# The first four row tiles of x: turned by TensorE, or by transposing transfers from SP

## The chip, the cores and the metric

One core of a Trainium2 chip. The metric is the device time of one execution in microseconds (us). The profile adds the span, from the first instruction of the program that it records to the last.

## The reference

Two linear-attention blocks, A and B, read the same x (2048 rows, D = 640, 32 heads of 20). B's own x is not used. Per block, in bf16:

```python
qkv = x @ wqkv                           # 640 -> 3 * 640
phi = lambda t: jnp.where(t > 0, t + 1, jnp.exp(t)) + 1e-6
pq, pk = phi(q), phi(k)
kv = jnp.einsum("bhsd,bhse->bhde", pk, v)
z = jnp.einsum("bhsd->bhd", pk)
o = (pq @ kv) / (pq . z + 1e-6)          # per head
block = o @ wo
```

The result mixes them by a gate: `g = sigmoid((x * gate_w).sum(-1))`, `out = g * a + (1 - g) * b`.

## The kernel before

The 2048 rows are 16 row tiles (chunks) of 128 and four row blocks of 512 (n = 0 to 3); the 640 columns of x are five slices of 128 (c = 0 to 4). Two copies of x lie in SBUF: `xn`, rows on partitions, and `xT`, columns on partitions (five slices of 2048). The products with wk and wq contract over columns and read `xT`; the later passes that build x^T pk (`g_pass`, `g_strassen`) read `xn`.

**What PE does, in order.** Seven warm-up matmuls on a constant (L172). The transpose of the gate row `grow` (5 x 128, in a corner of the tile `R`) into `gcol` (L174); DVE copies it to `gsb` and GpSimd puts it as a 641st column behind each slice of wkA (L178), so that the second k matmul of each slice (321 columns) also gives the gate's logits. Then `k_first` (L252), whose order is written out by hand: the first four chunks of `xn` are transposed on TensorE (`x_transpose`, L215), four times five transposes, and DVE copies the result into `xT` (L218, two copies for each chunk). Then k for chunks 0 to 3: 40 matmuls (L236; five slices, two halves of 320 columns, four chunks), slice 0 for all, slice 1 for all, then slices 2 to 4 chunk by chunk. `k_done` ends a chunk: ACT's exp (L223) and a copy of the logit column (L242), DVE's two operations of phi (L228, L232).

After that come q for row block 0 (`q_block` twice, `q_single`; L296, L306), k for chunks 4 to 7, q for block 1, k for the other chunks, q for blocks 2 and 3 (L285), and the later passes: the sums of x and pk, x^T pk by Strassen's scheme, the normalisers, all of B, and the output products (L607).

PSUM is held in four slots of two banks (`ps`, tags ps0 to ps3). The warm-up and `gcol` have slot 3, the turned chunks slots 0 and 1; the k products of chunks 0 to 3 have slots 2, 3, 0, 1.

**What the queues do.** SP and ACT issue the first transfers. ACT: the gate row, x tiles 1 and 3, wkA slice 1. SP: x tiles 0 and 2, wkA slice 0, slice 2, slices 3 and 4, then wqA in two parts (L136), then 15 transposing transfers (L139), which write `xT` for row blocks 1 to 3 straight from DRAM, five slices of 512 columns for each block. Later on SP: x rows of blocks 1 to 3 into `xn` (L738), wvA, woA (L695), wkB.

In row block 0, tile q holds the rows 4p + q (p = partition), and the stores of the result (`rows_of`) undo this.

Transfers of the hardware queues take turns on eight completion semaphores: the ninth waits for the landing of the first, and so on, on the queue that issues it.

GpSimd makes the constants first (identity, masks, `spread`, `I16`), then the gate columns, then clears part of `R` and fills `chosen`, both for a later pass.

Of the kernel before, what the change touches and what calls it, by code (L numbers as in the profile page):

```python
# [8 lines left out]
P = 128  # L9
FP32 = mybir.dt.float32  # L10
BF16 = mybir.dt.bfloat16
# [3 lines left out]
S, D, H = 2048, 640, 32  # L15
Dh = D // H
DT = D // P
ST = S // P
NB = 4
CB = 4  # L20
HB = 512
# [12 lines left out]
def kernel(  # L34
# [11 lines left out]
    nc = tc.nc  # L46
    x2 = A_x.flatten_outer_dims()
    out2 = out.flatten_outer_dims()
# [4 lines left out]
    work = ctx.enter_context(tc.tile_pool(name="work", bufs=2))  # L53
# [18 lines left out]
    xn = persist.tile([P, ST, D], BF16, name="xn")  # L72
# [6 lines left out]
    ident = persist.tile([P, P], BF16, name="ident")  # L79
# [5 lines left out]
    R = persist.tile([P, 2, 4, RB], BF16, name="R")  # L85
    ones = persist.tile([P, H], BF16, name="ones")
    I16 = persist.tile([P, ST], BF16, name="I16")
# [3 lines left out]
    hc, ic = ST // 2, 2 * P  # L91
# [14 lines left out]
    wq_dram = [A_wqkv.rearrange("(c p) f -> p c f", p=P), B_wqkv.rearrange("(c p) f -> p c f", p=P)]  # L106
# [3 lines left out]
    nc.vector.memset(ones[:], 1.0)  # L110
    nc.vector.memset(KVT[:], 0.0)
    nc.vector.memset(lift[:], 1.0 + EPS)
    xb0 = x2[0:CB * P, :].rearrange("(p q) d -> p q d", q=CB)
    wk = [None, None]
    wv = [None, None]
    wq = [None, None]
    wk[0] = wpool.tile([P, DT, D + 16], BF16, tag="wk", name="wkA")
    def load_x(eng, lo, hi):
        eng.dma_start(out=xn[:, lo:hi, :], in_=xb0[:, lo:hi, :])

    def load_wk(eng, lo, hi):
        eng.dma_start(out=wk[0][:, lo:hi, 0:D], in_=wq_dram[0][:, lo:hi, D:2 * D])

    grow, logitT = R[0:DT, 0, 2, 0:P], R[:, 0, 1, 0:P]
    nc.scalar.dma_start(out=grow, in_=gate_w.rearrange("(c p) -> c p", p=P))
    load_x(nc.sync, 0, 1)
    load_x(nc.scalar, 1, 2)
    load_x(nc.sync, 2, 3)
    load_x(nc.scalar, 3, 4)
    load_wk(nc.sync, 0, 1)  # L130
    load_wk(nc.scalar, 1, 2)
    load_wk(nc.sync, 2, 3)
    load_wk(nc.sync, 3, DT)
    wq[0] = wpool.tile([P, DT, D], BF16, tag="wq", name="wqA")
    for lo, hi in ((0, 2), (2, DT)):
        nc.sync.dma_start(out=wq[0][:, lo:hi, :], in_=wq_dram[0][:, lo:hi, 0:D])  # L136
    for n in range(1, NB):
        for c in range(DT):
            nc.sync.dma_start_transpose(  # L139
                out=xT[:, c, n * HB:(n + 1) * HB], in_=x2[n * HB:(n + 1) * HB, c * P:(c + 1) * P]  # L140
            )


    make_identity(nc, ident[:])
    for r in range(4):
        rows = slice(32 * r, 32 * r + 32)
        nc.gpsimd.tensor_copy(out=I4[rows], in_=ident[rows, rows])
    nc.gpsimd.tensor_copy(
        out=spread[:].rearrange("p (h t) -> p h t", t=TW), in_=I4[:, :, None].to_broadcast([P, H, TW])
    )  # L150
    nc.gpsimd.tensor_tensor(
        out=I16[0:2 * ST], in0=ident[0:2 * ST, 0:ST], in1=ident[0:2 * ST, ST:2 * ST], op=ALU.add
    )
    nc.gpsimd.memset(maskE[:], 1.0)
    for sign, base in ((1, 0), (-1, Dh - 1)):
        nc.gpsimd.affine_select(
            out=maskE[:], in_=maskE[:], pattern=[[-sign * Dh, WB[0] // Dh], [0, Dh]],
# [3 lines left out]
    for sign, base in ((1, 0), (-1, TW - 1)):  # L161
        nc.gpsimd.affine_select(
            out=headE[:], in_=headE[:], pattern=[[-sign * TW, H]],
# [1 line left out]
        )  # L165


    raw = ps_raw("warm", 3)
    warm = raw.bitcast(FP32).rearrange("p (b n) -> p b n", b=2)
    one_l, one_r = [nc.const_aps.tensor(1.0, [P, n], BF16) for n in (P, HB)]  # L170
    for k in range(7):
        nc.tensor.matmul(warm[:, 0, :], lhsT=one_l, rhs=one_r, start=True, stop=True)  # L172
    gcol = raw[:, 2 * HB:2 * HB + DT]
    nc.tensor.transpose(out=gcol, in_=grow, identity=ident[0:DT, 0:DT])  # L174
    gsb = work.tile([P, DT], BF16, tag="rT", name="gsb")
    nc.vector.tensor_copy(out=gsb[:], in_=gcol)
    for c in (0, 1, 2, 4, 3):
        nc.gpsimd.tensor_copy(out=wk[0][:, c, D:D + 1], in_=gsb[:, c:c + 1])  # L178

    def by_group(dst, lhsT, src, h):  # L180

# [27 lines left out]

    def gate_done(b):  # L210
        nc.vector.tensor_scalar(ge[b][:], ge[b][:], 1.0, 1e30, op0=ALU.add, op1=ALU.min)

    def x_transpose(i, pt, cuts=(0, DT)):
        for c in range(DT):
            nc.tensor.transpose(out=pt[:, c * P:(c + 1) * P], in_=xn[:, i, c * P:(c + 1) * P], identity=ident[:])  # L215
        src = pt[:, 0:D].rearrange("p (c n) -> p c n", c=DT)
        for lo, hi in zip(cuts, cuts[1:]):
            nc.vector.tensor_copy(out=xT[:, lo:hi, i * P:(i + 1) * P], in_=src[:, lo:hi])  # L218

    def phi(dst, src, n, lifted=False, side=None):  # L220

        e = work.tile([P, src.shape[1], n], BF16, tag="e", name="e", bufs=3)
        nc.scalar.activation(out=e[:], in_=src, func=ACT.Exp)  # L223
        if side is not None:
            side()
        if lifted:
            nc.scalar.activation(out=dst, in_=src, func=ACT.Identity, bias=lift[:])
        nc.vector.tensor_scalar(e[:], e[:], 1.0, EPS, op0=ALU.min, op1=ALU.add)  # L228
        if lifted:
            nc.vector.tensor_tensor(out=dst, in0=dst, in1=e[:], op=ALU.max)  # L230
            return
        nc.vector.scalar_tensor_tensor(out=dst, in0=src, scalar=1.0 + EPS, in1=e[:], op0=ALU.add, op1=ALU.max)  # L232

    def k_mm(b, i, c, pt, hf):
        w = HF + (hf if b == 0 else 0)
        nc.tensor.matmul(  # L236
            pt[:, hf, 0:w], lhsT=xT[:, c, i * P:(i + 1) * P], rhs=wk[b][:, c, hf * HF:hf * HF + w],
            start=(c == 0), stop=(c == DT - 1),
        )

    def k_done(b, i, pt):
        side = (lambda: nc.scalar.copy(out=logit[:, i:i + 1], in_=pt[:, 1, HF:HF + 1])) if b == 0 else None  # L242
        phi(pk[:, i, :].rearrange("p (b n) -> p b n", b=2), pt[:, :, 0:HF], HF, side=side)

    def k_chunk(b, i, slot=None):
        pt = ps(f"k{'AB'[b]}", slot)
        for hf in range(2):
            for c in range(DT):
                k_mm(b, i, c, pt, hf)
        k_done(b, i, pt)  # L250

    def k_first():  # L252

        pts = [ps("kA", 2 + i) for i in range(2)]
        raw = [ps_raw("xt", i) for i in range(2)]

        def part(i, cs):
            for c in cs:
                for hf in range(2):
                    k_mm(0, i, c, pts[i], hf)  # L260

        for i in range(4):
            x_transpose(i, raw[i % 2][:, i // 2 * 2 * HB:], (0, 2, DT))
        for i in range(2):
            part(i, (0,))
        pts += [ps("kA", i) for i in range(2)]
        for i in range(2, 4):
            part(i, (0,))
        for i in range(4):
            part(i, (1,))  # L270
        for i in range(4):
            part(i, (2, 3, 4))
            k_done(0, i, pts[i])

    def mixed(t, m):
# [320 lines left out]
        nc.vector.tensor_tensor(out=pqT[b][:, m, :], in0=pqT[b][:, m, :], in1=rec, op=ALU.mult)  # L596

    def rows_of(i):
        n, q = divmod(i, CB)
        rows = out2[n * HB:(n + 1) * HB, :]  # L600
        return rows.rearrange("(p q) d -> q p d", q=CB)[q] if n == 0 else rows[q * P:(q + 1) * P, :]

    def prod(dst, left, right, i, first):

# [12 lines left out]
    class Pair:  # L617
# [7 lines left out]
        def store(self, k, lo=0, hi=D):  # L625
            eng = nc.scalar if self.last and k else nc.sync
            eng.dma_start(out=rows_of(self.i + k * (ST // 2))[:, lo:hi], in_=self.osb[k][:, lo:hi])
# [89 lines left out]
    with tc.manual_schedule():  # L717
        k_first()
    turn[0] = 2
    nc.gpsimd.memset(R[:, :, 0:2, :], 0.0)  # L720
    chosen = R[:, 1, 0:2, :].rearrange("p a (b n) -> p (a b) n", b=2)
    for h in range(2):
        for q in range(2):
            i0 = h * hc + q
            nc.gpsimd.tensor_copy(
                out=chosen[0:2 * ST, 2 * h + q, :].rearrange("p (j n) -> p j n", j=4),
                in_=I16[0:2 * ST, i0:i0 + hc - 1:2][:, :, None].to_broadcast([2 * ST, 4, 32]),
            )
    for n in range(2):
        for i in range(CB if n else 0, CB * 2 * n):  # L730
            k_chunk(0, i)
# [2 lines left out]
        q_single(0, DT - 1, n)  # L734
    for i in range(hc, ST - 2):
        k_chunk(0, i)
    for n in range(1, NB):
        nc.sync.dma_start(  # L738
            out=xn[:, n * CB:(n + 1) * CB, :], in_=x2[n * HB:(n + 1) * HB, :].rearrange("(q p) d -> p q d", p=P)
        )  # L740
    wv[0] = load_w(0, "v", nc.sync)
    load_wo(0, nc.sync)
# [5 lines left out]
    def bank(pool, name, n=1):  # L748
        return pool.tile([P, HB] if n == 1 else [P, n, HB], FP32, tag=name, name=name)

    with tc.manual_schedule():
# [31 lines left out]
        part = [slice(n * RB, (n + 1) * RB) for n in range(4)]  # L783
# [17 lines left out]
        with late_pool("single") as single:  # L801
# [6 lines left out]
            pts = [bank(single, f"s4{hf}")[:, 0:HF] for hf in range(2)]  # L808
# [21 lines left out]
        for i in range(1, half):  # L830
            p, after = pairs[i], pairs[i + 1] if i + 1 < half else None
# [9 lines left out]
            q = after if i + 2 < half else p if after is None else None  # L841
# [43 lines left out]
```

## Time and profile before

| | |
|---|---|
| time, median of 3 runs | 188.69 us (188.54 to 188.95) |
| the profiled execution | 188.86 us |
| its span | 187.2 us |
| busy: PE, DVE, ACT, POOL | 183.1, 150.3, 76.3, 6.0 us |
| first k matmul, first q matmul of PE | 6.43, 11.97 us |
| last of wqA landed | 10.8 us |

The profile's chain is the work that ended last, followed back from the end. Times in it are us from the span's start. Matmuls overlap in the engine, so a row's duration for one matmul is longer than the distance between two starts; where one matmul's cost is meant, the distance counts. "DMA to landing" is the time from the start of an issue to the completion semaphore. DMA share is the mean busy share of 16 DMA engines; it passes 1 where pieces that are waiting in the engines count as busy. PEld is the weight load, which runs beside the matmul before it.

### The profile page before, as it was taken

The page shows a single profiled execution, that of the slowest core. Times are in us where ns is not written, and L with a number is a line of the kernel's source. Part 1 is how long each engine was busy: PE and PEld are TensorE (multiplying, and loading weights), DVE is VectorE, ACT ScalarE, POOL GpSimd, SP SyncE. Part 2 cuts the span into 40 slices and gives each one's busy share as a digit, 9 for nine tenths or more (in the row PEclk, how much of TensorE's full clock was granted, in tenths as well). Part 3 has the DMA queues.
Part 4 walks back from the last instruction along what each step waited for, and adds up shares of the span by engine and source line. Part 5 has one row for each costly group of instructions (what it writes and reads, how often), then busy time and mean ns, then how long its engine had stood idle before and what let it go on. Part 6 is the DMA issues. An engine that isn't in the chain of part 4 may idle for free.

```text
span 187.2 us, 3548 instructions
## 1 busy us (share of the span) xinstructions
PE 183.1 (98%) x1426; PEld 123.7 (66%) x1431; DVE 150.3 (80%) x247; ACT 76.3 (41%) x124; POOL 6.0 (3%) x30
## 2 busy tenths in 40 slices
PE   8999999999999999999999999999999999999993
PEld 3765757765577677877775555576777776777772
DVE  1468868889998998799889998739699989787554
ACT  2065545547962501367674577432401611111120
POOL 7400000010000000000000000000000000000000
PEclk9999999999999999999999999999999999999999
DMA  5993449972040000011115000000533002311132
GB/s 169 323 165 74 99 98 352 322 164 101 9 170 0 0 4 0 0 36 33 55 38 190 8 0 0 0 4 0 179 98 77 4 0 91 123 67 65 50 107 70
DMA packets 19173, 15.64 MB, mean 84 GB/s; under 512 B 8916, under 2 KB 19028, under 8 KB 19156
## 3 DMA queue, kind: packets, MB, share of 16 engines
q1 hardware_dynamic: 18426, 14.75, 28.0%
q10 hardware_dynamic: 730, 0.66, 1.1%
q8 instruction: 11, 0.18, 0.4%
q14 instruction: 6, 0.05, 0.1%
HBM read 10.00 MB, written 3.44 MB: 72 GB/s over the span
## 4 chain that ended last, share of the span: by engine, by line
PE 96%; DVE 2%; issue 0%; ACT 0%; DVEq 0%; ACTq 0%
PE gs L367 16%; PE kA L236 12%; PE kB L236 12%; PE qB L285 12%; PE ox L607 6%; PE qA L285 6%; PE oy L607 5%; PE oz L607 5%; PE qA L296 5%; PE ow L607 3%; PE gA L340 2%; PE gB L340 2%; PE warm L172 2%; PE qA L306 1%; DVE osb L612 1%; PE xt L215 1%
## 5 line engine op out<-in xcount | busy, mean ns | idle before, releaser
L236 PEld LDWEIGHTS <-xT 128*128 128x128 bf16 x320 | 31.1, 98 | 12.4 <-DVE xT L218 0.2
L228 DVE TENSOR_SCALAR e<-e 128x640 bf16<-128x640 bf16 (+2 forms) x53 | 18.9, 357 | 8.3 <-ACT e L223 7.6
L236 PE MATMUL kB<-wkB,xT 128*128 128x320 bf16 x160 | 23.0, 299 | 0.0
L236 PE MATMUL kA<-wkA,xT 128*128 128x320 bf16 (+1 forms) x160 | 22.4, 300 | 0.0
L285 PE MATMUL qB<-xT,wqB 128*128 128x512 bf16 x98 | 21.7, 379 | 0.1
L223 ACT ACTIVATE e<-kB 128x640 bf16<-128x640 f32 x16 | 11.3, 705 | 18.8 <-PE kB L236 17.5
L285 PEld LDWEIGHTS <-wqB 128*128 128x128 bf16 x100 | 11.7, 117 | 9.8 <-issue 0.2
L223 ACT ACTIVATE e<-kA 128x640 bf16<-128x640 f32 x16 | 11.3, 705 | 13.4 <-PE kA L236 13.3
L232 DVE SCALAR_TENSOR_TENSOR pk<-kA,e 128x640 bf16<-128x640 f32 x16 | 13.2, 824 | 2.1 <-DVE e L228 0.2
L232 DVE SCALAR_TENSOR_TENSOR pk<-kB,e 128x640 bf16<-128x640 f32 x16 | 13.2, 825 | 1.7
L223 ACT ACTIVATE e<-qB 128x1024 bf16<-128x1024 f32 x10 | 10.3, 1025 | 8.7 <-PE qB L285 8.3
L223 ACT ACTIVATE e<-qA 128x1024 bf16<-128x1024 f32 (+1 forms) x11 | 10.4, 948 | 8.1 <-PE qA L296 5.1
L651 ACT COPY u<-ox 128x320 f32<-128x320 f32 x8 | 3.4, 427 | 21.8 <-PE ox L607 21.8
L367 PEld LDWEIGHTS <-S 128*128 128x128 bf16 x96 | 9.4, 98 | 3.6
L367 PEld LDWEIGHTS <-xn 128*128 128x128 bf16 x96 | 9.1, 98 | 4.0 <-issue 0.4
L285 PE MATMUL qA<-xT,wqA 128*128 128x512 bf16 x49 | 10.9, 379 | 0.1
L635 ACT COPY p1s<-ox 128x320 f32<-128x320 f32 x8 | 3.4, 427 | 16.5 <-PE ox L607 16.5
L607 PEld LDWEIGHTS <-xT 128*128 128x128 bf16 x85 | 8.0, 98 | 3.1 <-DVE xT L546 0.2
L607 PEld LDWEIGHTS <-pqTA 128*128 128x128 bf16 x85 | 7.9, 98 | 2.9 <-issue 0.2
L607 PEld LDWEIGHTS <-pqTB 128*128 128x128 bf16 x80 | 7.8, 98 | 3.0
L367 PE MATMUL gs<-pk,xn 128*128 128x320 bf16 x64 | 9.4, 300 | 0.0
L612 DVE TENSOR_TENSOR osb<-oz,u 128x320 bf16<-128x320 f32 (+1 forms) x18 | 8.0, 452 | 1.5 <-PE oz L607 0.8
(138 smaller groups left out, 293.6 us busy)
## 6 DMA issues: line engine op xcount, KB each, us to landing
out_dram<-osb SPq DMA_DIRECT2D x14, 160.0 KB, 1.8
xn<-in_A_x_dram SPq DMA_DIRECT2D x3, 640.0 KB, 6.6
wvA<-in_A_wqkv_dram SPq DMA_DIRECT2D x1, 800.0 KB, 10.6
wkB<-in_B_wqkv_dram SPq DMA_DIRECT2D x1, 800.0 KB, 4.5
wqB<-in_B_wqkv_dram SPq DMA_DIRECT2D x1, 800.0 KB, 4.6
MA<-ma_dram SPq DMA_DIRECT2D x1, 800.0 KB, 5.0
wvB<-in_B_wqkv_dram SPq DMA_DIRECT2D x1, 800.0 KB, 4.6
woB<-in_B_wo_dram SPq DMA_DIRECT2D x1, 800.0 KB, 5.7
```

Source lines behind the costliest of these rows:

```text
L172: nc.tensor.matmul(warm[:, 0, :], lhsT=one_l, rhs=one_r, start=True, stop=True)
L223: nc.scalar.activation(out=e[:], in_=src, func=ACT.Exp)
L228: nc.vector.tensor_scalar(e[:], e[:], 1.0, EPS, op0=ALU.min, op1=ALU.add)
L232: nc.vector.scalar_tensor_tensor(out=dst, in0=src, scalar=1.0 + EPS, in1=e[:], op0=ALU.add, op1=ALU.max)
L236: nc.tensor.matmul(pt[:, hf, 0:w], lhsT=xT[:, c, i * P:(i + 1) * P], rhs=wk[b][:, c, hf * HF:hf * HF + w], start=(c == 0), stop=(c == DT - 1),
L285: nc.tensor.matmul(pt[:, u, :], lhsT=mixed(wq[b][:, c, :], m), rhs=xT[:, c, n * HB:(n + 1) * HB], start=(c == 0), stop=(c == DT - 1),)
L296: nc.tensor.matmul(pt[:, u, :], lhsT=mixed(wq[b][:, c, :], m + u), rhs=xT[:, c, n * HB:(n + 1) * HB], start=(c == 0), stop=(c == DT - 1),)
L340: nc.tensor.matmul(pt[:, hf, 0:HF], lhsT=xn[:, i, c * P:(c + 1) * P], rhs=pk[:, i, hf * HF:(hf + 1) * HF], start=(i == 0), stop=(i == ST - 1),
L367: nc.tensor.matmul(pt[:, n, 0:HF], lhsT=left[:, i, n * P:(n + 1) * P], rhs=right[:, i, :], start=(first and i == 0), stop=(i == hc - 1), s ...
L607: nc.tensor.matmul(dst, lhsT=left[:, c, r0:r0 + P], rhs=right[:, c, :], start=(first and c == 0), stop=(c == DT - 1), skip_group_check=not ...
L612: nc.vector.tensor_tensor(out=dst, in0=acc, in1=sb, op=ALU.add)
L635: nc.scalar.copy(out=self.p1s[:], in_=self.at("x"))
```

## The change

Only row tile 0 of x is loaded to `xn` at the start and goes through TensorE: five transposes, three DVE copies with the one of the gate column between them. Rows 128 to 511 come transposed, by five transfers of 384 columns that are the first that SP issues. x tile 0 is the first on ACT; behind it all of wkA in three transfers (slice 0; 1 and 2; 3 and 4) and wqA's slices 0 and 1. wqA's slices 2 to 4 are on SP after the five. The gate row is loaded by GpSimd, and its transpose on PE stands behind those of x.

The order of the k matmuls in `k_first` changes: slice 0 by halves, chunks 1, 2, 3, 0; slice 1 for all chunks; the rest of chunk 0, which is then ended; slices 2, 3, 4 for chunks 1 to 3, each ended after its slice 4. The warm-up and `gcol` have slot 1, the turned tile slot 2. Clearing `R` and filling `chosen` moves into `k_first`, behind the gate columns on GpSimd. Rows are in plain order everywhere, so `rows_of` is simple; rows 128 to 511 are loaded into `xn` with the other blocks' rows, in a transfer of their own before theirs.

```diff
-    xb0 = x2[0:CB * P, :].rearrange("(p q) d -> p q d", q=CB)
-    def load_x(eng, lo, hi):
-        eng.dma_start(out=xn[:, lo:hi, :], in_=xb0[:, lo:hi, :])
+    def x_turned(c, lo, hi):
+        nc.sync.dma_start_transpose(out=xT[:, c, lo:hi], in_=x2[lo:hi, c * P:(c + 1) * P])
...
-    nc.scalar.dma_start(out=grow, in_=gate_w.rearrange("(c p) -> c p", p=P))
-    load_x(nc.sync, 0, 1)
-    load_x(nc.scalar, 1, 2)
-    load_x(nc.sync, 2, 3)
-    load_x(nc.scalar, 3, 4)
-    load_wk(nc.sync, 0, 1)
-    load_wk(nc.scalar, 1, 2)
-    load_wk(nc.sync, 2, 3)
-    load_wk(nc.sync, 3, DT)
...
-    for lo, hi in ((0, 2), (2, DT)):
-        nc.sync.dma_start(out=wq[0][:, lo:hi, :], in_=wq_dram[0][:, lo:hi, 0:D])
+    nc.gpsimd.dma_start(out=grow, in_=gate_w.rearrange("(c p) -> c p", p=P))
+    nc.scalar.dma_start(out=xn[:, 0, :], in_=x2[0:P, :])
+    for c in range(DT):
+        x_turned(c, P, HB)
+    for lo, hi in ((0, 1), (1, 3), (3, DT)):
+        load_wk(nc.scalar, lo, hi)
+    for eng, lo, hi in ((nc.scalar, 0, 2), (nc.sync, 2, DT)):
+        eng.dma_start(out=wq[0][:, lo:hi, :], in_=wq_dram[0][:, lo:hi, 0:D])
     for n in range(1, NB):
         for c in range(DT):
-            nc.sync.dma_start_transpose(
...
+            x_turned(c, n * HB, (n + 1) * HB)
...
-    raw = ps_raw("warm", 3)
+    raw = ps_raw("warm", 1)
...
     def k_first():
...
+        xt = ps_raw("xt", 2)
+        for c in range(DT):
+            nc.tensor.transpose(out=xt[:, c * P:(c + 1) * P], in_=xn[:, 0, c * P:(c + 1) * P], identity=ident[:])
+        nc.tensor.transpose(out=gcol, in_=grow, identity=ident[0:DT, 0:DT])
+        gsb = work.tile([P, DT], BF16, tag="rT", name="gsb")
+        src = xt[:, 0:D].rearrange("p (c n) -> p c n", c=DT)
+        nc.vector.tensor_copy(out=xT[:, 0:2, 0:P], in_=src[:, 0:2])
+        nc.vector.tensor_copy(out=gsb[:], in_=gcol)
+        nc.vector.tensor_copy(out=xT[:, 2:DT, 0:P], in_=src[:, 2:DT])
+        for c in range(DT):
+            nc.gpsimd.tensor_copy(out=wk[0][:, c, D:D + 1], in_=gsb[:, c:c + 1])
...
+        pts = {i: ps("kA", (2 + i) % 4) for i in (1, 2, 3, 0)}
+        for hf in range(2):
+            for i in (1, 2, 3, 0):
+                k_mm(0, i, 0, pts[i], hf)
...
-        for i in range(4):
-            x_transpose(i, raw[i % 2][:, i // 2 * 2 * HB:], (0, 2, DT))
...
+        for i in range(CB):
             part(i, (1,))
-        for i in range(4):
-            part(i, (2, 3, 4))
+        part(0, (2, 3, 4))
+        k_done(0, 0, pts[0])
+        for i in range(1, CB):
+            part(i, (2,))
+        for i in range(1, CB):
+            part(i, (3,))
+        for i in range(1, CB):
+            part(i, (4,))
             k_done(0, i, pts[i])
...
-    for n in range(1, NB):
+    for n in range(NB):
+        lo, hi = max(n * CB, 1), (n + 1) * CB
         nc.sync.dma_start(
-            out=xn[:, n * CB:(n + 1) * CB, :], in_=x2[n * HB:(n + 1) * HB, :].rearrange("(q p) d -> p q d", p=P)
+            out=xn[:, lo:hi, :], in_=x2[lo * P:hi * P, :].rearrange("(q p) d -> p q d", p=P)
         )
```

More of the change, by code (lines that the diff above doesn't have):

```diff
@@ L124 @@
     grow, logitT = R[0:DT, 0, 2, 0:P], R[:, 0, 1, 0:P]
-    nc.scalar.dma_start(out=grow, in_=gate_w.rearrange("(c p) -> c p", p=P))
-    load_x(nc.sync, 0, 1)
-    load_x(nc.scalar, 1, 2)
-    load_x(nc.sync, 2, 3)
-    load_x(nc.scalar, 3, 4)
-    load_wk(nc.sync, 0, 1)
-    load_wk(nc.scalar, 1, 2)
-    load_wk(nc.sync, 2, 3)
-    load_wk(nc.sync, 3, DT)
-    wq[0] = wpool.tile([P, DT, D], BF16, tag="wq", name="wqA")
-    for lo, hi in ((0, 2), (2, DT)):
-        nc.sync.dma_start(out=wq[0][:, lo:hi, :], in_=wq_dram[0][:, lo:hi, 0:D])
+    wq[0] = wpool.tile([P, DT, D], BF16, tag="wq", name="wqA")
+    nc.gpsimd.dma_start(out=grow, in_=gate_w.rearrange("(c p) -> c p", p=P))
[6 more added lines that the diff above has]
+        eng.dma_start(out=wq[0][:, lo:hi, :], in_=wq_dram[0][:, lo:hi, 0:D])
     for n in range(1, NB):
         for c in range(DT):
-            nc.sync.dma_start_transpose(
-                out=xT[:, c, n * HB:(n + 1) * HB], in_=x2[n * HB:(n + 1) * HB, c * P:(c + 1) * P]
-            )
+            x_turned(c, n * HB, (n + 1) * HB)
     make_identity(nc, ident[:])
@@ L173 @@
     gcol = raw[:, 2 * HB:2 * HB + DT]
[L174 to L178, printed above, removed]
+    chosen = R[:, 1, 0:2, :].rearrange("p a (b n) -> p (a b) n", b=2)
     def by_group(dst, lhsT, src, h):
@@ L211, in gate_done @@
         nc.vector.tensor_scalar(ge[b][:], ge[b][:], 1.0, 1e30, op0=ALU.add, op1=ALU.min)
[L213 to L218, printed above, removed]
     def phi(dst, src, n, lifted=False, side=None):
@@ L252, in k_first @@
     def k_first():
-        pts = [ps("kA", 2 + i) for i in range(2)]
-        raw = [ps_raw("xt", i) for i in range(2)]
+        xt = ps_raw("xt", 2)
[9 more added lines that the diff above has]
+            nc.gpsimd.tensor_copy(out=wk[0][:, c, D:D + 1], in_=gsb[:, c:c + 1])
+        nc.gpsimd.memset(R[:, :, 0:2, :], 0.0)
+        for h in range(2):
+            for q in range(2):
+                i0 = h * hc + q
+                nc.gpsimd.tensor_copy(
+                    out=chosen[0:2 * ST, 2 * h + q, :].rearrange("p (j n) -> p j n", j=4),
+                    in_=I16[0:2 * ST, i0:i0 + hc - 1:2][:, :, None].to_broadcast([2 * ST, 4, 32]),
+                )
+        pts = {i: ps("kA", (2 + i) % 4) for i in (1, 2, 3, 0)}
+        for hf in range(2):
+            for i in (1, 2, 3, 0):
+                k_mm(0, i, 0, pts[i], hf)
         def part(i, cs):
@@ L260, in part @@
                     k_mm(0, i, c, pts[i], hf)
-        for i in range(4):
-            x_transpose(i, raw[i % 2][:, i // 2 * 2 * HB:], (0, 2, DT))
[L264 to L268, printed above, removed]
-        for i in range(4):
-            part(i, (1,))
-        for i in range(4):
-            part(i, (2, 3, 4))
+        for i in range(CB):
+            part(i, (1,))
+        part(0, (2, 3, 4))
[6 more added lines that the diff above has]
+            part(i, (4,))
             k_done(0, i, pts[i])
@@ L598, in rows_of @@
     def rows_of(i):
-        n, q = divmod(i, CB)
-        rows = out2[n * HB:(n + 1) * HB, :]
-        return rows.rearrange("(p q) d -> q p d", q=CB)[q] if n == 0 else rows[q * P:(q + 1) * P, :]
+        return out2[i * P:(i + 1) * P, :]
     def prod(dst, left, right, i, first):
@@ L719 @@
     turn[0] = 2
[L720 to L728, printed above, removed]
     for n in range(2):
```

## The prediction

> **What bounds the kernel now.** I read the page first: the busy shares, then the chain that ended last.
>
> ```profile
> span 187.2 us, 3548 instructions
> PE 183.1 (98%) x1426; PEld 123.7 (66%) x1431; DVE 150.3 (80%) x247; ACT 76.3 (41%) x124; POOL 6.0 (3%) x30
> ...
> PE 96%; DVE 2%; issue 0%; ACT 0%; DVEq 0%; ACTq 0%
> ```
>
> PE carries 96% of the chain. What is saved on PE moves the end one for one, as long as nobody else becomes late. The change touches the start, so I read the chain of its first 30 us in order of time (start, length, what):
>
> ```profile
> 0.84 3.15 PE warm L172 x7
> 3.99 0.12 PE warm L174
> 4.11 0.65 PE xt L215 x5
> ...
> 6.59 5.54 PE kA L236 x40
> 12.14 0.22 PE qA L296
> ...
> 12.40 4.05 PE qA L296 x18
> ```
>
> After seven warm-up matmuls PE turns four chunks of x (20 transposes), then runs the 40 k matmuls of the first four chunks, then q. In the timeline of PE the k matmuls start at 6.43 and the first q matmul at 11.97. All later PE work follows without a gap over 0.3 us up to 181.6. So the one number that matters is when q can start.
>
> Next, how fast the transfers of the start arrive (windows: PE, PEld, DVE, ACT, POOL, clock, DMA share, GB/s; the first groups cover copies alone, then copies with transposes, then transposes alone, first backlogged and then steady):
>
> ```profile
> 1.80:5.00 3.20, 3.16 (x15) 1.22 (x14) 0.37 (x3) 1.28 (x1) 2.46 (x16) 1.00 0.97 281
> 5.00:9.00 4.00, 3.94 (x34) 2.85 (x33) 1.96 (x8) 0.00 (x0) 1.90 (x6) 1.00 0.97 323
> 9.00:10.50 1.50, 1.50 (x14) 1.08 (x12) 0.04 (x1) 0.76 (x2) 0.00 (x0) 1.00 1.54 157
> 10.50:12.00 1.50, 1.50 (x14) 1.10 (x12) 1.34 (x3) 1.40 (x4) 0.00 (x0) 1.00 1.31 262
> 15.50:26.00 10.50, 10.45 (x64) 6.66 (x64) 8.32 (x14) 5.48 (x11) 0.00 (x0) 1.00 0.40 88
> ```
>
> Last, the transposing transfers when little else runs (first line: 15.7 to 26 us) and the weight loads of PE's transposes (late line: window 6.12 to 6.45, early line: 4.7 to 5.95):
>
> ```profile
> L139 SPq DMA_TRANSPOSE xT<-in_A_x_dram x8: 1258/1260/1262, 15.6 to 24.7; - x8
> ...
> DMA to landing us min/median/max: 2.7/2.7/2.8
> ```
> ```profile
> L215 PEld LDWEIGHTS <-xn x4: 96/96/97, 6.2 to 6.3; 128*128 128x128 bf16 x4
> ```
> ```profile
> L215 PEld LDWEIGHTS <-xn x11: 104/151/152, 4.8 to 5.8; 128*128 128x128 bf16 x11
> ```
>
> SP spends 1.26 us to issue 512 columns, and they land 2.7 us after the issue began. PE is slow until about 6.0: seven 512-column matmuls take 3.15 us (0.43 each) against 4.05 for 18 (0.22). The slow clock is half.
>
> **Part by part.**
>
> *Fifteen PE transposes and six DVE copies go.* Five are left. They start at 3.92 (xn row tile 0 is first on ACT; the first x tile on SP landed at 3.05 after issue at 0.81) and are spaced 0.107 as in the slow stretch, to 4.46; the gate row's transpose, now behind them, ends its slot at 4.57. There k may start, 1.86 us earlier than 6.43.
>
> *The first k matmuls are slow or wait.* At half clock a 320-column matmul takes 0.27 (twice 0.136). The tiles of chunks 1 and 2 go at 4.57 and 4.84. Chunk 3 takes the bank that holds the gate row until DVE has copied it. DVE: copy of two slices 4.75 to 5.05, gate 5.05 to 5.21 (0.16 each, L176), three slices to 5.56 (0.35, L218). So chunk 3 starts at 5.25, and chunk 0, whose bank held the turned tile, at 5.60. The second half of slice 0 waits for the gate column on POOL (0.19 each after 5.21, so about 5.45); PE comes there at 5.87. With the clock up at 6.0, slice 0 is done at 6.48. The other 32 matmuls at 0.1365 (row 6.43 to 11.97 for 40 is 0.1385 with its two small gaps) take 4.37: q starts at 10.85 instead of 11.97. **Gain 1.12 us.** Of the 1.86, 0.74 is given back to the slow clock and to DVE's copies.
>
> *Five transposing transfers of 384 columns, first on SP.* Issue: between 0.95 (three quarters of 1.26) and 1.26 (nothing shrinks); I take 1.05, near the proportional end. Issues start at 0.81, 1.9, 3.0, 4.1, 5.2; with 2.6 to 3.2 to landing (2.7 seen, some more beside copies) they land at about 3.8, 4.9, 6.0, 7.0, 8.1. PE asks for them at 4.57, 6.75, 8.4, 9.2, 10.0. Cost nothing, with 0.8 us to spare at the tightest, the first. If the cover goes, each 0.1 late costs 0.1.
>
> *wkA on ACT alone.* In the built order the third transfer (slices 3 and 4) waits on ACT for the landing of transpose 0, and wqA's first part behind it for transpose 1, since the transfers of all hardware queues take turns on eight semaphores. Behind these on ACT stand the table load (1.28, now at about 5.5 instead of 2.75) and the first exp, asked for at 8.4. Slack 1.5. Bytes in ring order at the 281 and 323 GB/s above: wkA slice 0 lands at 4.2 (asked 4.57), slices 1 and 2 at 5.4 (6.48), 3 and 4 at 7.0 (7.84).
>
> *wqA on two queues.* x tile 0 0.16 MB, five transposes 0.49, wkA 0.82, wqA 0.82: 2.29 MB from 1.83 on. By the two rates it is in at 9.3 and lands at about 9.6; before, the last of wqA landed at 10.8. q's third matmul asks for the second part at 11.3. It must come in at 250 GB/s to be in time; this is the narrowest condition.
>
> *Later transposes on SP.* Behind the five and wqA they start at 6.75 instead of 5.17. The last of block 1 starts at 12 to 12.7 and lands by 15.5 (before: 10.68 and 13.88); PE asks at 17.9 - 1.1 = 16.8. Blocks 2 and 3, the x rows (now with tiles 1 to 3, 480 KB more), wvA and woA follow about 1.6 later with many us of cover (x rows landed by 35.1, asked for at 50).
>
> *Gate row by POOL.* No POOL transfer is in the trace. Its issue is bounded by 0.56 (the same transfer on ACT) and 1.68 (the longest issue of a plain copy, woA): ident then is ready at 2.1 to 3.2, before 3.92. Its landing: 2.2 us after issue (first x tile) to 6.2 (wqA behind a full queue), so 3.0 to 7.0; I take 3.0 to 4.2, as it is 1.25 KB. At 7.0 PE would stand 2.4 us.
>
> [...]
>
> *Sum.* The profiled execution took 188.86: 187.2 of span and 1.66 around it. Span 186.1, execution 187.74. It stood 0.17 above the median 188.69, so **187.6**.
>
> **Rivals.**
>
> *Copies and transposes side by side run slowly (slower, 0.20).* For: from 9.0 to 10.5, where both were in flight, only 157 GB/s moved, at a DMA share of 1.54. Against: there the transposes stood behind 0.8 MB of wqA in one ring; now they are at the head. The condition is a rate: at 250 GB/s q is on time, at 221 (2.29 MB by 12.2) the old time comes back, below it is slower. At 200, wqA lands at 13.6 against 12.4, when q's third matmul ran before: 189.9. At 157 throughout it lands at 16.7: 193.
>
> *The clock comes up later (slower, 0.07).* Full speed came some 5.1 us after the first matmul; PE's start is now thinner, with waits of 0.15 and 0.1 and, if transpose 0 is late, more. Each us that the full clock comes later costs 0.5: it decides from 2.2 us on (8.2). One more stretch of 3.15 us, the warm-up's length, with the wait that caused it (0.7): 188.69 - 1.12 + 1.6 + 0.7 = 189.9. [...]
>
> *The gate row lands late (slower, 0.05).* PE stands in front of all k matmuls. Past a landing at 5.7 the gain is gone; at 7.0 it is 190.0.
>
> *A partial wait eats the gain (no change, 0.07).* wqA at 12.4, or transpose 4 at 11.2 instead of 8.1. That one transpose landed 6.1 us after issue behind a full ring is the row for it: 5.2 + 6.1 = 11.3.
>
> That the change does not do what it says is no rival: the order of SP's and ACT's transfers is as written.
>
> **How the numbers follow.** 0.2% (0.38 us) is about what the runs of before, 188.54 to 188.95, can tell from no change. The forecast with its own range (187.0 to 188.3, from an earlier full clock, worth 0.2, and run spread, to 0.7 us of late data) has 0.61. No change 0.07. Slower 0.20 + 0.07 + 0.05 = 0.32. The range is 187.0 to 190.0: it takes in the rivals to about their middle and leaves out some 0.17, the worst of the slow rates and late gate rows.
>
> **What would show it.** Right: k matmuls from 4.5 to 4.7, first q matmul at 10.7 to 11.0, no q wait on wqA, transposes landing 2.6 to 3.2 after issue. Wrong: PE weight loads at L219 waiting on transfers of xT or wkA, a q weight load waiting on wqA, weight loads of 151 ns past 7 us, or PE waiting on R.

## The result: slower by 0.85%, and the profile after

| | before | after |
|---|---|---|
| time, median of 6 runs of each on one chip | 188.62 us (188.23 to 191.20) | 190.21 us (189.60 to 190.47) |
| the profiled execution | 188.86 us | 190.47 us |
| its span | 187.2 us | 188.8 us |
| first k matmul, first q matmul of PE | 6.43, 11.97 us | 4.74, 12.40 us |

The ratio after to before is 1.0085, with a 95% interval of 1.0063 to 1.0107. The forecast was 187.6 us, faster: it had the wrong sign. Between the two profiled executions (after's is the slowest of its six) lie 1.61 us, and the trace places them: q starts 0.49 us later in the steady row, and another 1.1 us come 140 us into the kernel, at a place for which the prediction had no term.

The page of after, its span, busy row and chain by engine:

```profile
span 188.8 us, 3515 instructions
PE 182.7 (97%) x1411; PEld 122.6 (65%) x1416; DVE 148.7 (79%) x241; ACT 76.0 (40%) x124; POOL 6.7 (4%) x31
...
PE 90%; SPq 3%; DMA 3%; DVE 2%; issue 0%; ACT 0%; DVEq 0%; ACTq 0%
```

PE works 0.4 us less than before and yet the span is longer, so what was added is waiting. SPq (SP issuing DMAs) and DMA are new in the chain. That chain from the last of SP's five transposing transfers on (start, length, what):

```profile
5.94 1.25 SPq L118
7.19 0.04 issue
7.24 5.58 DMA wqA<-in_A_wqkv_dram
12.82 0.05 issue
12.87 4.08 PE qA L299 x18
```

Before, this stretch of the chain was PE, but for the end of a DVE copy (to 6.11). Now the path to q's third matmul runs through SP: five issues of transposing transfers, one behind the other from 0.81 on, then wqA's second part, which lands at 12.82. PE's timeline shows what else stood in the way (start, length, instructions, and in brackets the idle time in front and what ended it):

```profile
4.74 3.27 PE L219 MATMUL kA<-wkA,xT 128*128 128x320 bf16 x18
8.16 1.52 PE L219 MATMUL kA<-wkA,xT 128*128 128x320 bf16 x10 [0.16 <-DMA wkA<-in_A_wqkv_dram]
9.99 0.99 PE L219 MATMUL kA<-wkA,xT 128*128 128x320 bf16 x6 [0.31 <-DMA xT<-in_A_x_dram]
11.57 0.99 PE L219 MATMUL kA<-wkA,xT 128*128 128x320 bf16 x6 [0.59 <-DMA xT<-in_A_x_dram]
12.40 4.55 PE L299 MATMUL qA<-xT,wqA 128*128 128x512 bf16 x19
```

k starts early, as forecast, and then waits: for wkA's last part, for slice 3 of `xT`, for slice 4. Slice 4 lands at 11.53, so k ends and q begins at 12.40. q's third matmul followed its first by 0.43 before; after, it could have run at 12.83, and wqA held it to 12.87. So of the 0.49 nearly all is slice 4's. A second execution of the same kernel (e7 below) has the fifth transposing transfer itself in its chain:

```profile
5.94 5.60 DMA xT<-in_A_x_dram
...
11.59 0.99 PE kA L219 x6
```

The five transposing transfers on SP, their issue (ns, least, median, most) and their way to landing:

```profile
L118 SPq DMA_TRANSPOSE xT<-in_A_x_dram x5: 1218/1244/1252, 0.8 to 5.9; - x5
...
DMA to landing us min/median/max: 3.5/4.1/5.6
```

Two windows of after (PE, PEld, DVE, ACT, POOL, clock, DMA share, GB/s) show when the data failed to come:

```profile
5.00:6.50 1.50, 1.50 (x9) 0.91 (x8) 0.18 (x1) 0.00 (x0) 1.50 (x6) 1.00 1.00 134
7.50:10.00 2.50, 2.04 (x15) 1.11 (x13) 0.33 (x1) 1.11 (x3) 0.07 (x1) 1.00 0.82 92
```

Between 5.0 and 6.5, and between 7.5 and 10.0, only 134 and 92 GB/s moved. The same stretches before:

```profile
5.00:6.50 1.50, 1.44 (x16) 1.22 (x15) 1.27 (x6) 0.00 (x0) 1.44 (x5) 1.00 0.91 273
7.50:10.00 2.50, 2.50 (x20) 1.73 (x18) 0.00 (x0) 0.28 (x1) 0.00 (x0) 1.00 1.49 304
```

The second figure varies between executions of the same kernel: e7 moved 153, 310 and 204 GB/s from 5.0, 6.5 and 7.5 on, so 92 is not typical.

Now the late place, in the chain of time. Before:

```profile
138.89 2.72 PE gs L367 x20
141.61 0.77 PE mid L461 x20
```

After:

```profile
138.97 3.14 PE gs L370 x23
142.11 0.02 issue
142.13 0.90 DVE GT L425 x2
143.03 0.04 issue
143.08 0.92 PE mid L464 x20
```

`mid` (L461, L464) is the first product of the last part. Before, it followed the last `gs` product without a pause, beside DVE's last two operations on `gs`; now PE waits until they are done. In the timelines `mid` starts at 141.45 before and at 143.08 after: 1.63 later, of which 0.49 had come from the start. The other 1.14 arise here.

### The profile page after: what moved, and what is told of

The parts are those of the page before. It is cut to its first block, busy times and chain, and to the rows that moved or that the text cites. A ratio compares the mean times of both kernels' runs of the same rounds, so it can differ in the third digit from the quotient of the medians.

```text
span 188.8 us, 3515 instructions
## 1 busy us (share of the span) xinstructions
PE 182.7 (97%) x1411; PEld 122.6 (65%) x1416; DVE 148.7 (79%) x241; ACT 76.0 (40%) x124; POOL 6.7 (4%) x31
## 4 chain that ended last, share of the span: by engine, by line
PE 90%; SPq 3%; DMA 3%; DVE 2%; issue 0%; ACT 0%; DVEq 0%; ACTq 0%
PE gs L370 16%; PE kB L219 12%; PE qB L288 11%; PE kA L219 9%; PE ox L608 6%; PE qA L288 6%; PE oy L608 5%; PE oz L608 5%; PE qA L299 4%; SPq L118 3%; DMA wqA<-in_A_wqkv_dram 3%; PE ow L608 3%; PE gB L343 2%; PE gA L343 2%; PE qA L309 1%; DVE osb L613 1%
## 5 line engine op out<-in xcount | busy, mean ns | idle before, releaser
L219 PE MATMUL kA<-wkA,xT 128*128 128x320 bf16 (+1 forms) x160 | 23.5, 305 | 1.1 <-DMA xT<-in_A_x_dram 0.9
L206 ACT ACTIVATE e<-kB 128x640 bf16<-128x640 f32 x16 | 11.2, 703 | 18.9 <-PE kB L219 18.2
L206 ACT ACTIVATE e<-kA 128x640 bf16<-128x640 f32 x16 | 11.2, 707 | 11.1 <-PE kA L219 11.1
```

What stands on the lines that cost most here:

```text
L219: nc.tensor.matmul(pt[:, hf, 0:w], lhsT=xT[:, c, i * P:(i + 1) * P], rhs=wk[b][:, c, hf * HF:hf * HF + w], start=(c == 0), stop=(c == DT - 1),
```

## The theories

**Banks.** By this theory, PSUM slots (tags ps0 to ps3) get their banks in the order in which the program first names them. The bank numbers below are the author's, worked out from it; no trace shows them. Before: 3, 2, 0, 1. After: 1, 2, 3, 0, since the warm-up took slot 1 and the turned tile slot 2. So slot 0, which holds the last `gs` tile (`even` in L425's pass), moved from banks 4 and 5 to 6 and 7. The last part has a pool of its own, whose first `mid` product lies in banks 6 and 7 in both kernels. Before, these held the other tile of the pass (`odd`), which DVE reads earlier (139.47 to 140.29 in the trace of before, with `mid` from 141.45); after, they hold the `gs` tile that DVE is still reading (142.13 to 143.02, with `mid` from 143.08).

**Supply.** At the start, the transposing transfers are slow to issue and slow to land, and wkA's third transfer is issued only once transpose 0 has landed (4.71).

**Rival to supply: bytes and pieces alone.** The same bytes in the same 256 B pieces would arrive as late without any turning.

**Rival to both: the clock.** PE waits in its first microseconds, and full speed comes later.

## The experiments

All ratios are against the kernel before, on the same chip. The medians of before were 188.96 (first four runs), 189.19 (next four), 189.32 (next two) and 189.17 us (last). A ratio need not be the quotient of two medians.

### The old banks in the new kernel, and the new banks in the old one

`e1_banks_as_before` is the changed kernel with the slots first named in the old order, just ahead of `def ps`; `e2_before_new_banks` is the old kernel with them named in the new order.

```diff
+    for s in (3, 2, 0, 1):        # e1; in e2: (1, 2, 3, 0)
+        ps_raw("bank", s)
```

> The changed kernel, with the four PSUM slots first named in the order of the kernel before (3, 2, 0, 1), so that each slot has its old banks; nothing else differs. Banks theory: 1.1 of the 1.6 us lost come from the wait of PE at 142 us, where the first product of the last part (tile mid, second pair of banks) now lies in the banks that DVE is still reading (gs, even). With the old banks that wait is gone: 189.1 us, and the first q matmuls still 0.4 to 0.5 late. Rival, all of the loss comes from the start or its later echo (late wkB, wvB): 190.2 us, and PE still waits near 142.

> The kernel before, with the slots first named in the order of the changed kernel (1, 2, 3, 0). Banks theory: 188.6 + 1.1 = 189.7 us, with PE waiting about 1.1 near 141.5 for DVE's reading of gs, and nothing different in the first 30 us. Rival (start or its echo): 188.6 us, no wait.

e1: 189.26 us, ratio 1.0014 (0.9982 to 1.0046). e2: 190.18 us, ratio 1.0061 (1.0022 to 1.0099). The order of four names alone makes the old kernel 1.2 us slower. In its timeline `mid` starts 1.34 later than before. Of that, 0.21 is there already when q starts (12.18); no difference was expected there, and its cause is open. So the late place is worth 1.13. The chain has the same wait there:

```profile
141.85 0.90 DVE GT L425 x2
142.75 0.04 issue
142.79 0.92 PE mid L464 x20
```

e1's own profiled execution, at 191.31 the second slowest of its twelve runs, has no such wait, but another loss (its chain of the start):

```profile
4.98 4.69 DMA wkA<-in_A_wqkv_dram
9.67 0.04 issue
9.71 4.83 PE kA L222 x22
```

PE stood 2.08 us for wkA's last part, and the 22 matmuls behind that took 0.22 us each instead of 0.14: the clock had fallen (0.69 granted from 10.0 to 12.5). That speaks for the rival of the clock in some executions, so the comparison was repeated.

### After and e1 side by side again

`e7_after_again` is the changed kernel, `e8_banks_again` is e1.

> The changed kernel, unaltered, beside the others on one chip. Banks theory: 1.1 above e8; above before by 1.4 to 1.7.

> e1 once more, beside the changed kernel: the difference of the two is the banks' share alone. Banks theory: 1.1 below the changed kernel (1.0 to 1.3), 0.3 to 0.6 above before. In the profile k goes on from 8 to 12 us at full clock (in e1's profile the clock had fallen and the matmuls from 9.7 us took 0.22 each). Rival: no difference to the changed kernel beyond 0.4.

e7: 190.30 us, ratio 1.0065 (1.0038 to 1.0091). e8: 189.17 us, ratio 0.9988 (0.9963 to 1.0014). The banks alone are worth 1.13 us, what the trace had given (1.14). With the old banks the change can't be told from before. The 0.3 to 0.6 above before that were expected for e8 are not in its median (189.17 against 189.19). Its profiled execution, at 189.65 the second slowest of twelve, does have q 0.77 us late; so what the start costs varies with the execution. The chain of e8 at the late place:

```profile
138.98 3.40 PE gs L373 x25
142.37 0.77 PE mid L467 x20
```

So the theory of the banks is shown in both directions: the names move 1.1 us and PE's wait with them. What stays is the other half of the question: where the gain of 1.12 us at the start went. All the runs that follow have the old banks.

### Plain pieces instead of transposes

`e3_plain_pieces` replaces the five transposing transfers by plain copies of the same 256 B pieces. The turning is left out, so `xT` of rows 128 to 511 holds x as it is.

```diff
+        if lo == P:
+            nc.sync.dma_start(
+                out=xT[:, c, lo:hi].rearrange("p (q d) -> p q d", d=P),
+                in_=x2[lo:hi, c * P:(c + 1) * P].rearrange("(q p) d -> p q d", p=P),
+            )
+            return
```

> As e1, but the five transfers of x rows 128 to 511 on SP are plain copies of the same 256 B pieces, 384 each, to the same place: the turning is left out. Mixing theory (transposing transfers beside copies hold up the DMA engines): from 5 to 10 us the engines move 280 GB/s or more, k waits for no x slice after 6 us, q starts near 10.9: 187.5 us. Rival, it is the small pieces, or what two queues ask for at once: rates of 100 to 150 GB/s remain in some stretches, and the time is within 0.3 of e1. A part of any gain is the shorter issue on SP (0.4 instead of 1.25 each).

188.51 us, ratio 0.9976 (0.9953 to 1.0000). Two windows of e3:

```profile
5.00:6.50 1.50, 1.22 (x8) 0.53 (x7) 0.31 (x2) 0.94 (x1) 1.39 (x6) 1.00 0.98 294
7.50:10.00 2.50, 2.50 (x21) 1.81 (x19) 0.00 (x0) 0.67 (x2) 0.20 (x1) 1.00 1.39 357
```

The hole in the supply is gone: 294 GB/s from 5.0 to 6.5, where six executions with the transposing transfers and wkA in three parts have 124 to 153, and 357 from 7.5 on, where they have 92 to 256. But two things went at once. The transfers now take the eight semaphores in another order, and wkA's third transfer, which waited for transpose 0 until 4.55 to 5.00 in those six, is issued at 2.23 without a wait. So from e1 to e3 the turning, the long issues and that wait all go at once. The time, 0.75 us below e1, missed what was expected (187.5): the plain copies are issued so fast (0.45 to 0.49 us each for the same pieces in e11) that wqA is issued at 3.8 to 4.3 and is in flight beside the rest, wkA's slices 1 and 2 landed only at 7.18, PE waited 1.0 us for them, and q started at 11.58. Rate alone is not enough; the order of arrival counts too.

### wqA behind the transposes

`e4_wqA_on_SP` has both parts of wqA on SP, so that they can't get ahead of wkA. `e5_no_wait_for_wk` was to name wkA's loads between the transposes as well, to take away the wait of wkA's third transfer for transpose 0.

```diff
-    for eng, lo, hi in ((nc.scalar, 0, 2), (nc.sync, 2, DT)):
+    for eng, lo, hi in ((nc.sync, 0, 2), (nc.sync, 2, DT)):
```

> As e1, but both parts of wqA are on SP behind the five transposes, so that the last transposes have no wqA copies beside them. Mixing theory: slices 3 and 4 land at about 8.3 and 9.6 instead of 9.9 and 11.5, wqA's second part at 11.0 to 11.5, the third q matmul runs at about 11.5 instead of 12.9: 187.8 to 188.6 us. Rival (bytes alone set it): wqA comes later, as it starts later, and the time is that of e1 or up to 0.5 above.

> As e4, with wkA's transfers named between the first three transposes, so that the last part of wkA (slices 3 and 4) gets a free semaphore and no longer waits on ACT for transpose 0 to land (5.0 us in e4); x tile 0's semaphore, free since 3.3, is taken by a later transfer instead. If that wait keeps k back: wkA lands near 7.5 instead of 8.9, PE's wait of 1.0 before the rest of chunk 0 is gone, q starts 0.5 to 0.9 earlier: 187.8 to 188.2 us. If holding up by transposes beside copies sets the pace whatever the order: the transposes of slices 1 to 4 come later by about what wkA gains, and the time is that of e4, 188.4 to 188.8.

e4: 188.60 us, ratio 0.9982 (0.9959 to 1.0006). e5: 188.61 us, ratio 0.9962 (0.9937 to 0.9987). e5 did not do what it was made for: in the built order wkA's last part still waits for transpose 0 and is issued at 4.77, so it says nothing on that wait and is e4 once more. In e4 transposes 3 and 4 land at 9.13 and 9.35, in e5 at 8.81 and 9.12 (e1: 10.12 and 11.58; e8: 9.90 and 10.26), so without wqA's copies beside them they do come earlier, as the mixing theory said; e4's time is at the upper end of its 187.8 to 188.6. The chain of e5, from 0.81:

```profile
0.81 3.94 DMA xT<-in_A_x_dram
4.75 0.02 issue
4.77 3.85 DMA wkA<-in_A_wqkv_dram
8.62 0.04 issue
8.66 3.16 PE kA L223 x22
```

Here q starts at 11.66, 0.3 earlier than before (in e4 at 11.93). This is the fastest version by the median that still turns the rows: one of its two measurements is faster by a little under 0.4%, the other can't be told from before.

### The transfers by themselves

`e6_bench_at_end` is the old kernel with five stages behind its end, where nothing else runs: (1) the five transposes, (2) three copies of 320 KB on ACT, (3) both, (4) plain pieces in place of the transposes, (5) pieces and copies.

> The kernel before with five stages added behind its end, each begun by small memsets that wait for the stage before; the added transfers write into tiles that nobody reads any more, so the result is as before, and the time is longer by the stages. Stage 1: the five 384-column transposing transfers alone (SP). 2: three copies of 320 KB alone (ACT). 3: both at once. 4: five plain transfers of the same 256 B pieces alone (SP). 5: these and the copies at once. Mixing theory: 1 takes 8 us (five issues of 1.25 and 1.6 to land), 2 takes 5.5, 3 takes 11 or more, clearly over the longer of the two, with copies stuck in the engines for 0.5 us or more each; 4 takes 4, 5 takes about 7 (1.47 MB at 280 GB/s and 1.9). Rival (bytes and pieces alone): 3 takes 8 to 8.5 and the copies of stage 3 land within 1.5 of stage 2.

From the first issue to the last landing the stages took 7.6, 5.1, 7.9, 4.45 and 7.1 us. The windows of the third and the fifth stage without their first microsecond:

```profile
200.00:207.00 7.00, 0.00 (x0) 0.00 (x0) 0.00 (x0) 0.00 (x0) 0.00 (x0) 0.50 0.92 211
213.20:219.40 6.20, 0.00 (x0) 0.00 (x0) 0.00 (x0) 0.00 (x0) 0.00 (x0) 0.50 0.90 238
```

In quiet, the copies cost the transposes 0.3 us in all, and 211 against 238 GB/s is no collapse. The mixing theory had asked for 11 us in the third stage; what came is near the rival's 8 to 8.5. A single transpose that lands 2.4 to 2.5 us after its issue began alone takes 2.8 to 5.3 beside copies, and the copies' landings go from 2.9 to 4.1 up to 3.1 to 5.2. But a plain transfer of the same pieces does the same: 2.1 to 2.4 alone, 3.6 to 5.4 beside copies. What differs is the issue, 1.14 to 1.20 us each in the first stage against 0.40 to 0.49 in the fourth, and that accounts for the first stage's longer time (7.6 against 4.45). So this run, a single one, shows later landings with or without turning, and not the rates of 134 and 92.

### wkA in two transfers

With wkA in two transfers (slices 0 and 1; 2 to 4) the second has a free semaphore and waits for nothing. `e9_wk_in_two` does that; `e10_wk_in_two_wqA_on_SP` also puts wqA on SP as in e4.

```diff
-    for lo, hi in ((0, 1), (1, 3), (3, DT)):
+    for lo, hi in ((0, 2), (2, DT)):
```

> As e1 (old banks, wqA on two queues), but wkA comes in two transfers (slices 0 and 1; 2 to 4) instead of three, so that none of it waits on ACT for transpose 0; only wqA's first part still does. Gap theory (the low rates of 120 to 150 GB/s at 5 to 6.5 us come from the ring running empty while wkA's last part waits to be issued): over 250 GB/s in that stretch, wkA all landed by 7.2, the transposes of slices 3 and 4 by 9 to 9.8, q starts near 10.5 to 11: 187.3 to 187.9 us. Mixing theory (transposes beside copies hold the engines up): under 180 GB/s there still, wkA's last part lands after 8, q starts at 11.9 or later: 188.6 to 189.2.

> As e9, and both parts of wqA on SP behind the transposes, as in e4. Gap theory: wkA by 7.2, slices 3 and 4 by 8.3 and 9.0, k ends by 10; wqA, issued from 7.2 on, lands at 10.5 and 12.0 as in e4 and sets the start of q's third matmul: 188.0 to 188.3, a little worse than e9. Mixing theory: better than e9, as the last transposes have no copies beside them, and within 0.3 of e4 (188.6).

e9: 188.81 us, ratio 0.9986 (0.9958 to 1.0013). e10: 188.82 us, ratio 0.9987 (0.9951 to 1.0024). Both missed what closing the gap was to give (187.3 to 187.9, and 188.0 to 188.3). wkA now lands at 6.74 and 6.57, and the rate from 5.0 to 6.5 rises from 133 in e1 to 205 and 221, which is still not 294. e9's window, then its chain to the end of k:

```profile
5.00:6.50 1.50, 0.81 (x4) 0.46 (x5) 0.39 (x2) 0.43 (x1) 1.31 (x6) 1.00 1.45 205
```
```profile
0.81 4.84 DMA xT<-in_A_x_dram
5.65 0.05 issue
5.69 7.41 PE kA L222 x40
```

In this execution of e9 PE waited 0.22 us for the gate row and 0.77 for transpose 0 ahead of the first k matmul; then all 40 ran without a wait, in 7.41 us instead of 5.54. Their weight loads say why:

```profile
L222 PEld LDWEIGHTS <-xT x14: 104/151/152, 5.7 to 8.9; 128*128 128x128 bf16 x14
```

151 ns is the slow clock, here until about 9.3 and not 6.0 (the column of the granted clock shows 1.00 all the while). This execution took 189.91, one of the three slowest of its twelve; nine lie within 188.54 to 188.94, and no trace shows what held those. In e10, whose profiled execution (188.70) is near its median, wkA was in at 6.57 and all five transposes by 8.80; k's last 30 matmuls ran from 7.08 without a wait, and q began at 11.18. Its third matmul then waited for wqA:

```profile
7.87 4.06 DMA wqA<-in_A_wqkv_dram
...
11.97 4.08 PE qA L302 x18
```

Before, that row stood at 12.40, so q's steady part runs 0.43 us earlier; 0.2 of it is left at the end of the span (187.0 against 187.2). With the gap closed and wqA last, the transposing transfers held k for only 0.48 us (slice 1). What they still cost is SP's time: five issues from 0.81 to 7.19, and only then wqA.

### Two transfers and plain pieces

`e11_two_plain` is e9 with the plain pieces of e3: neither gap nor transposing transfers. (The text on record says that e3 still had the gap; as shown above, it had not, so e11 differs from e3 in wkA's parts alone.) The turning is left out as there.

> As e9_wk_in_two (banks as before; wkA in two transfers, slices 0 and 1, then 2 to 4, so that no transfer of wkA waits for the landing of a transpose), and the five transposes replaced by plain copies of the same 256 B pieces, with the turning left out (xT of rows 128 to 511 then holds x not turned). It parts the two things that were changed apart so far: the turning (e3 against e1) and the wait in wkA's issue (e9 against e1). Theory, the turning itself holds the engines in the first microseconds: without a gap in the supply and without turning, the rate from 5.0 to 6.5 is 290 GB/s or more (e9 had 205, e3 with the gap 294), no piece is held over 0.5 us between 5.6 and 6.5, wkA's last part lands by 6.5 and the five by 7.0. Rival, copies and small pieces compete whatever the small pieces do: 190 to 240 GB/s in that stretch, as e9, and landings as in e9 (6.74; 7.2 to 9.3). On the time: k's matmuls then have all data early; if only the data held k, first q matmul at 10.9 to 11.4 and 187.6 to 188.3 us; if the clock takes it as in e9 (40 k matmuls in 7.41 us), q at 12.3 to 13 and 188.6 to 189.2.

188.49 us, ratio 0.9986 (0.9950 to 1.0022; ten runs, seven within 187.83 to 188.71 and three from 189.49 to 190.13). The profiled execution took 188.07. Its window, and PE's timeline:

```profile
5.00:6.50 1.50, 1.21 (x8) 0.70 (x9) 0.43 (x2) 0.53 (x1) 0.78 (x7) 1.00 1.04 304
```
```profile
5.29 0.17 PE L249 MATMUL warm<-ident,R 5*128 5x5 bf16 x1 [0.77 <-DMA R<-in_gate_w_dram]
5.40 5.80 PE L228 MATMUL kA<-wkA,xT 128*128 128x320 bf16 x40
11.04 3.22 PE L308 MATMUL qA<-xT,wqA 128*128 128x512 bf16 x14
```

304 GB/s against 205 in e9: the expected of the theory (290 or more), not of the rival (190 to 240), and nothing of 256 B was held over 0.5 us between 5.6 and 6.5. The landings missed it, though: wkA's last part came at 7.41 and the five from 3.82 to 8.39, as wqA was issued at 3.5 and was in flight beside them. In e10, which turns the rows but has wqA last, wkA was in at 6.57 and the last of the five at 8.80. By the packets of the two traces the 256 B pieces moved at the same rate from 5.0 to 6.5 (87 GB/s in e9, 86 in e11); it is the copies that went from 126 to 221, and e11 had more of them in flight (wqA issued at 3.54 and 3.84, in e9 at 5.67 and 7.23). So a higher rate here is in part only an earlier request. q starts at 11.04, 0.93 earlier than before, and this execution was 0.79 faster. So with the data there in time, PE's part of the forecast holds, and it reaches the end almost one for one. In the medians nothing sure is left of it: 188.49 against e9's 188.81, on two chips, and both have a ratio of 0.9986 to before. What the transposing transfers cost with the gap closed is not shown; the 0.75 between e1 and e3 holds the gap too.

## Why the prediction was wrong, point by point

**"What is saved on PE moves the end one for one, as long as nobody else becomes late."** The condition failed at a place that was not searched. The prediction followed PE to 181.6 and found no gap over 0.3, but asked of the moved slots only when the banks of `gcol` and of the turned tile come free at the start. Whose banks the slots were for the rest of the kernel it costed at nothing. Measured: 1.13 us (e7 against e8), 1.2 us (e2). This term was missing; it is most of the loss of 1.59. Of the 2.6 us between 187.6 and 190.21 it is 1.1; the other 1.5 are at the start, where q came at 12.40 and not at 10.85, and there the step that failed is the landing of the transposing transfers (below).

**k from 4.57.** Nearly right: 4.74. xn's first tile landed at 3.22, and five transposes followed as described; the gate row kept k back a little (below).

**The slow clock to about 6.0 and 0.1365 for a k matmul.** Right in after (99 ns for a weight load from 6.0 on), and e11's 40 matmuls in 5.64 show the sum on PE to be about right: from 4.57, 6.28 had been forecast, with its waits for DVE.

**The transposes' issue, 1.05.** Mis-sized: 1.22 to 1.25 for 384 columns. Of the two bounds, 0.95 and 1.26, the upper was the truth: a quarter fewer columns save 0.02. So the fifth issue began at 5.94 and not at 5.2, and wqA behind it at 7.24. A plain copy of the same pieces is issued in 0.45 to 0.49 (e11).

**Their landing, 2.6 to 3.2 after issue.** Mis-sized: 3.5 to 5.6. Landings were 4.69, 6.13, 6.87, 9.95 and 11.53, against 3.8, 4.9, 6.0, 7.0 and 8.1 in the sum. 2.7 came from rows of transposes that ran alone; e6 shows 2.4 alone and up to 5.3 beside copies. PE wanted the last at 10.0; it came 1.53 late, and q 1.55. By the prediction's own rule ("each 0.1 late costs 0.1") this is all that was lost at the start. In e6's quiet a single one lands nearly as soon as a plain one (2.4 to 2.5 us from the start of the issue against 2.1 to 2.4); a row from one queue does not, as the five took 7.6 us and the same pieces copied plainly 4.45.

**wkA in at 7.0.** 8.12. The prediction had named the wait of the third transfer for transpose 0 and given it no price; with transpose 0 at 4.69 instead of 3.8 it was issued at 4.71, and until 6.5 all transfers together moved 134 GB/s. In after this cost PE only 0.16; in e1 and e8, with the same queues, 2.08 and 0.77.

**wqA in at 9.6, "the narrowest condition".** 12.82. "2.29 MB by the two rates" took a rate of full queues for a stretch in which a queue was waiting to issue. But it was not the narrowest: k itself ended at 12.40, and wqA cost q's third matmul some 0.04 us more.

**The gate row, landed at 3.0 to 4.2.** 4.46 in after: GpSimd's issue began at 1.29 and not near 0.8, and 3.2 us passed to the landing. The weight load of its transpose waited 0.25 us for it, and k began 0.17 later than forecast. In e9 and e11 it took 3.4 and 3.95 and cost PE 0.22 and 0.77: the estimate was a little too early.

**The rivals.** For the start, the nearest on record was "a partial wait eats the gain" (no change, 0.07): it had transpose 4 at 11.2, which came at 11.53, and with the old banks the change is no change (e8). "Copies and transposes side by side run slowly" had low rates as its mechanism, and its time at 200 GB/s, 189.9, lies close to the 190.21 measured. But it lies there by chance, since the start cost only 0.43 to 0.49 and the banks the rest. What makes the start slow is in part the gap (133 to 205 GB/s when it is closed, e1 and e9). The rest (205 to 304, e9 and e11) goes with the transposing transfers, by their issue or by their turning. "Bytes and pieces alone" would have left the rate at the start as it was, and falls there; in e6's quiet it is what came. Of the signs of being wrong, three came: k's weight loads waited for transfers of `xT` (0.64 and 0.92 us), q's for wqA (0.34), and PE waited for `R`. "The clock comes up later" did not happen in after, but cost 1.7 us in the profiled execution of e1 (22 matmuls in 4.83 against e8's 3.16) and 1.9 in e9's (7.41 against 5.54), where full speed came at 9.3 instead of 6.0.

**What stays open.** Whether the transposing transfers hold back the copies by their long issue (1.25 against 0.48, so that SP's queue runs dry) or by their turning in the engines isn't parted: e3 and e11 change both. For the issue speak e6, where the landings are alike, and e10, where the five were all in by 8.80 and only wqA, behind their issues, was late; for the turning, that 256 B pieces were held 0.53 to 0.95 us between 5.6 and 6.6 in e9 and none over 0.02 in e11. Nor is it settled why the mix of e6's third stage keeps 211 GB/s while the start falls to 134 and 92; in after, 1280 B pieces on ACT's queue were held 0.85 to 1.54 us between 8.3 and 9.9 (in e7, the same kernel, none over 0.7 up to 10), in the bench no piece over 0.62. The wait of wkA's third transfer was still there in e5, so no run takes it away with all else left as it was: e9 and e10 change wkA's parts too.

## What to carry to other kernels

When a change renames or reorders PSUM slots, work out which banks each slot gets, and look at who reads those banks last and who writes them first, up to the end of the kernel: here the order of four names cost more than all that happened in the place that was changed. A forecast on arriving data is made transfer by transfer, from the issue (with what it waits for) to the landing beside the other traffic, and not from the bytes and a mean rate of full queues. And when PE is given work earlier, ask if its data lets it run without a pause: in e9's profiled execution, behind waits of 0.22 and 0.77 us, the slow clock lasted 3.3 us longer and the k matmuls took 1.9 more. It need not be so: e11, behind one wait of 0.77, ran its 40 in 5.64.

## What the runs showed of the hardware that was not expected

- A transposing transfer is issued in 1.22 to 1.25 us for 384 columns at the start (1.14 to 1.20 alone, e6) and 1.26 for 512 (before); a plain copy of the same pieces in 0.40 to 0.49 (e6, e11).
- Beside copies, a transposing transfer landed up to 5.3 us after its issue began in quiet (e6), 5.6 at the start of after and 6.15 in e8, instead of 2.4 to 2.5 alone. Plain ones of the same pieces went from 2.1 to 2.4 up to 5.4 in e6.
- PE ran slowly until 9.3 us in e9 while the granted clock read 1.00; the weight loads (151 ns, then 98) show it, the column does not. Nor does it show the slow first 6 us: before has 1.00 there too, at 0.43 us for a matmul that later takes 0.22.
- The clock need not fall in a wait: in e8 PE waited 0.75, 0.52 and 0.77 us (until 6.76, 7.71 and 9.75), and its last 22 k matmuls still took 3.16 us, 0.14 each; in e1, behind a wait of 2.08, they took 4.83.
